# GpSimd's elementwise work during attention, whole tiles before and half tiles after

## The chip, the cores and the metric

The kernel runs on one core of a Trainium2 chip. The core has five engines with instruction queues of their own: TensorE (PE in the profile, its weight loads PEld), VectorE (DVE), ScalarE (ACT), GpSimd (POOL) and SyncE (SP, which here issues nearly all DMAs). Each engine works its queue in order, and engines wait for each other through semaphores. The metric is the device time of one launch in microseconds (us), lower is better.

## The reference, cut to what matters

Attention with a threshold, and then two dense layers, each with an activation of its own, all in float32:

```
scores = q @ k.T / sqrt(64)                      # 4 batches, 8 heads, 576 x 576, head size 64
keep   = scores >= max(scores, -1) - tau
attn   = exp(scores - max) * keep ;  attn /= sum(attn, -1) + 1e-9
x      = (attn @ v)  -> (2304, 512)
h      = x @ w_in  (512 x 2048);   g = where(h >= 1, h, where(h <= -1, 0, (h + 1)**2 / 4));  y = g @ w_out
h      = y @ w_in2 ;               g = h * clip(h + 3, 0, 6) / 6 ;                           out = g @ w_out2
```

## The kernel before, in words

Attention is cut into 16 jobs, one for each batch and pair of heads, and a job into five blocks of query rows. For a block TensorE multiplies `kt` and `qt` into two PSUM banks (L328). VectorE moves each bank to SBUF as `p` and takes the row maximum on the way (L341). ScalarE takes the exponential `e` (L353). VectorE forms the threshold `th` (L356), and multiplies `e` by the mask into `p`, with the row sum as a second output (L362, the instruction with two SBUF inputs that returns throughout the text). TensorE transposes `p` (L277), ScalarE evicts the transposed tiles (L390, L404), and TensorE multiplies them by `v` (L426). When a job is over, VectorE takes the reciprocals of its row sums (L445, L446, L449), these go through DRAM to come back broadcast as `rb`, and GpSimd multiplies the job's output `xu` by `rb` (L481). From the fifth job on q and k are transposed by VectorE (L286, L302), and GpSimd scales the transposed queries by 0.125 (L288).

Every float32 weight is split into a high and a low part that TensorE takes in a fast format, and a product is three matmuls. The split of one 128x512 weight tile goes through three engines in turn: ScalarE (L118, L121), GpSimd clamps (L122), VectorE shifts (L129) and joins signs (L135), GpSimd adds the integer parts (L137), ScalarE rounds to the high part (L139), GpSimd subtracts to get the low part (L141). While attention runs, 20 such tiles are split.

After the first batch's four jobs the first dense layer begins on the finished columns, interleaved with the remaining attention. A step of it is twelve matmuls (L666) into a bank, ScalarE's L675 and L676, VectorE's L677 (one PSUM and one SBUF input) into `r`, ScalarE's rounding `gh` (L683), GpSimd's `gl` (L684), and twelve matmuls with the outgoing weights (L728). When attention is over, the rest of the first layer and the second one follow, in wider tiles (L666 and L708).

The order on each engine isn't written by hand: the program is recorded, and a list scheduler with a model of each instruction's time lays the queues out, within the dependences, a few priorities, and added dependences ("after") that keep some pace. What one instruction is thought to take thus moves others, on all engines.

Of the kernel before, what the change touches and what calls it, by code (L numbers as in the profile page):

```python
# [11 lines left out]
ALU = mybir.AluOpType  # L12
U32 = mybir.dt.uint32
I32 = mybir.dt.int32
# [4 lines left out]
def kernel(  # L19
# [13 lines left out]
    V, S, G, T = nc.vector, nc.scalar, nc.gpsimd, nc.tensor  # L33
    NB, NH, SEQ, D = q.shape
# [29 lines left out]
    taus = const.tile([128, 4], F32, name="taus")  # L64
# [9 lines left out]
    def f32(ap):  # L74
        return ap.bitcast(F32)
# [26 lines left out]
    def after(ins, prev, sync=False):  # L102
        if prev is not None:
            kind = mybir.DependencyClass.Sync if sync else mybir.DependencyClass.NoSync
            why = mybir.DependencyReason.ANTI if sync else mybir.DependencyReason.DATA
            tc.add_manual_dep(ins.ins, prev.ins.name, mybir.DependencyInfo(kind, why), reason="pace")

    pe_pins = []
    pins = {"S": None, "V": None, "G": None}

    def split_a(kind, m, f):
        t = wraw.pop((kind, m, f))
        pool = wbase if f < NF1 else wpool[f]
        hi = pool.tile([128, 512], F32R, tag=f"w{kind}h{f}", name=f"w{kind}h{f}")
        lo = pool.tile([128, 512], F32R, tag=f"w{kind}l{f}", name=f"w{kind}l{f}")
        c = stage.tile([128, 512], U32, tag="w_c", name="w_c", bufs=2)
        r = t[:, :, 0].bitcast(I32)
        x = S.activation(out=r, in_=t[:, :, 0], func=ACTF.Copy, scale=2.0 ** -29)  # L118
        after(x, pins["S"])
        if mode["att"]:  # L120
            after(S.activation(out=f32(c), in_=f32(t[:, :, 1]), func=ACTF.Abs), x)  # L121
            G.tensor_scalar(  # L122
                out=f32(c), in0=f32(c), scalar1=122879.9921875, scalar2=2.0 ** -15, op0=ALU.min, op1=ALU.max)
        else:
            S.activation(out=f32(c), in_=f32(t[:, :, 1]), func=ACTF.Abs)
            x = V.tensor_scalar(
                out=f32(c), in0=f32(c), scalar1=2.0 ** -15, scalar2=122879.9921875, op0=ALU.max, op1=ALU.min)
            after(x, pins["V"])
        V.tensor_scalar(out=c, in0=c, scalar1=3, scalar2=0x3FFFFFFF,  # L129
                        op0=ALU.logical_shift_left, op1=ALU.bitwise_and)  # L130
        wc[kind, m, f] = (hi, lo, c, t, r)

    def split_b(kind, m, f):
        hi, lo, c, t, r = wc.pop((kind, m, f))
        V.scalar_tensor_tensor(out=c, in0=t[:, :, 1], scalar=0xC0000000, in1=c,  # L135
                               op0=ALU.bitwise_and, op1=ALU.bitwise_or)
        x = G.tensor_tensor(out=c.bitcast(I32), in0=c.bitcast(I32), in1=r, op=ALU.add)  # L137
        after(x, pins["G"])
        x = S.activation(out=hi, in_=f32(c), func=ACTF.Copy)  # L139
        after(x, pins["S"])  # L140
        x = G.tensor_tensor(out=lo, in0=f32(c), in1=f32(hi), op=ALU.subtract)  # L141
        after(x, pins["G"])
        wsp[kind, m, f] = (hi, lo)

    wc = {}
# [1 line left out]
    class Weights:  # L147
# [16 lines left out]
        def half(self):  # L164
            if self.done < len(self.items):
                it = self.items[self.done]
                if not self.mid:
                    self.prefetch()
                    split_a(*it)
                else:  # L170
                    split_b(*it)
                    self.done += 1
                    self.prefetch()
                self.mid = not self.mid
# [32 lines left out]
    mode = {"mlp": False, "att": True, "step": False, "t": 0, "s": 0, "n": 0}  # L207
# [4 lines left out]
    qt, kt = {}, {}  # L212
# [17 lines left out]
    def load_q(j):  # L230
        if j >= NJ:
            return
        E = nc.sync if j else nc.scalar
        b, hp = jobs[j]
        for h in HEADS:
            src = q[b, 2 * hp + h]
            if j >= JT:
                strips(qn, 0, src, h)
                continue
            E.dma_start(out=qn[:, 0:4, h * D:(h + 1) * D], in_=rows(src, b))  # L240
            E.dma_start(out=qn[0:TAIL, 4, h * D:(h + 1) * D], in_=src[MAIN:SEQ, :])
# [15 lines left out]
    def load_v(j):  # L257
        if j >= NJ:
            return
        b, hp = jobs[j]  # L260
        t = vn[j % 2]
        for h in HEADS:
            src = v[b, 2 * hp + h]
            nc.sync.dma_start(out=t[:, 0:4, h, :], in_=rows(src, b))
            nc.sync.dma_start(out=t[h * TAIL:(h + 1) * TAIL, 4, h, :], in_=src[MAIN:SEQ, :])
# [3 lines left out]
    def unit_bank():  # L269
        mode["s"] += 1  # L270
        return pair_bank(f"P{mode['s'] % 2}")

    def reads(x, ago=0):
        readers[(mode["s"] - ago) % 2] = x

    def turn(out, in_, pin):
        x = T.transpose(out, in_, ident)  # L277
        if pin:
            pe_pins.append(x)

    def unit_q(j):
        if j >= NJ or j in qt:
            return
        qt[j] = ap.tile([128, SEQ], F32, tag="qt", name="qt", bufs=2)
        if j >= JT:
            V.transpose(out=qt[j], in_=qn.rearrange("p c n -> p (c n)")[:, 0:SEQ])  # L286
            load_q(j + 1)
            G.tensor_scalar(out=qt[j], in0=qt[j], scalar1=taus[:, 1:2], scalar2=None, op0=ALU.mult)  # L288
            return
        tm = unit_bank().rearrange("p e n -> p (e n)")  # L290
        for c in range(5):
            turn(tm[:, c * 128:(c + 1) * 128], qn[:, c, :], c == 0)
        load_q(j + 1)
        reads(S.activation(out=qt[j], in_=tm[:, 0:SEQ], func=ACTF.Copy, scale=taus[:, 1:2]))
# [118 lines left out]
    def pv_chunk():  # L413

        j, g, c = pvq.pop(0)
        n, d0 = GROUPS[g]
        f, t = gt[g, j]
        if c == 0:
            if j not in xu:
                here.pop(j - XLIVE, None)  # L420
                xu[j] = here[j] = mt.tile([128, SEQ], F32, tag="xu", name="xu", bufs=XLIVE)
            o_t[j, g] = rotate() if mode["mlp"] else bank("Q1")
        o = o_t[j, g][:, 0:n]
        for h in (1, 0):
            with tc.high_priority(offset=0 if h else 900):
                mm = T.matmul(o[h * D:(h + 1) * D], vn[j % 2][:, c, h, :], f[:, h, c] if c < 4 else t,  # L426
                              start=(c == 0), stop=(c == 4), skip_group_check=True)
            after(mm, pe_pins[-1] if h else prev)
            prev = mm
        if c == 4:  # L430
            del gt[g, j], o_t[j, g]
            S.activation(out=xu[j][:, d0:d0 + n], in_=o, func=ACTF.Copy)
# [38 lines left out]
    def em_norm(j):  # L471
        if j not in rbs:
            return
        while any(x[0] == j for x in pvq):
            pv_chunk()
        b, hp = jobs[j]
        rz, rb = rbs.pop(j)
        if j in OVER:
            load_v(j + 2)
            x = xu.pop(j)  # L480
            G.tensor_tensor(out=x, in0=x, in1=rb, op=ALU.mult)  # L481
            done_jobs.add(j)
            if b < NB - 1:
                nc.sync.dma_start(out=xd[b][:, hp, :], in_=x[:, 0:MAIN])
            nc.sync.dma_start(out=xd[NB][:, hp, b * TAIL:(b + 1) * TAIL], in_=x[:, MAIN:SEQ])
            return
        bm = unit_bank().rearrange("p e n -> p (e n)")
        for c in range(4):
            T.transpose(bm[:, c * 128:(c + 1) * 128], rb[:, c].rearrange("p h n -> p (h n)"), ident)
        load_v(j + 2)  # L490
        bt = bm[:, 512:640]
        T.transpose(bt, rz[:, 8, :].to_broadcast([128, 128]), ident)
        x = xu.pop(j)
        reads(V.tensor_tensor(out=x[:, 0:MAIN], in0=x[:, 0:MAIN], in1=bm[:, 0:MAIN], op=ALU.mult))
        done_jobs.add(j)
        if b < NB - 1:
            nc.sync.dma_start(out=xd[b][:, hp, :], in_=x[:, 0:MAIN])
        for h in HEADS:
            r = slice(64 * h, 64 * h + 64)
            reads(V.tensor_tensor(out=x[r, MAIN:SEQ], in0=x[r, MAIN:SEQ], in1=bt[r, 64 * h:64 * h + 64], op=ALU.mult))  # L500
        nc.sync.dma_start(out=xd[NB][:, hp, b * TAIL:(b + 1) * TAIL], in_=x[:, MAIN:SEQ])
# [3 lines left out]
    def attention():  # L505
# [36 lines left out]
        for t in range(n + 6):  # L542
            mode["t"] += 1
            mode["step"] = True
            if not mode["mlp"]:
# [18 lines left out]
                for x in now_at("q"):  # L564
                    unit_q(*x)
                    yield
# [15 lines left out]
            else:  # L582
# [18 lines left out]
                for x in now_at("q"):  # L601
                    unit_q(*x)
                    yield
# [186 lines left out]
    while o < len(outs):  # L790
        n = len(steps)
# [138 lines left out]
    for _ in attention():  # L930
# [11 lines left out]
        while credit > 0:  # L942
            c = next(part1)
# [98 lines left out]
```

## Time and profile before

| | us |
|---|---|
| median of 3 runs | 1124.85 (1124.29 to 1128.67) |
| the profiled execution | 1126.53 |
| its span | 1124.7 |
| PE busy in the span | 1086.1 |
| DVE, ACT, POOL busy | 586.9, 614.3, 435.5 |

The span is what the trace covers; 1.8 us of the profiled execution lie around it, and the execution itself is 1.7 us over the median. PE is busy 97% of the span, and the 40-slice picture shows where it isn't: in the first eight slices (some 225 us) it stands at 7 to 9 tenths, while DVE stands at 7 to 9 as well, and from there to the last slice it is full. The granted clock is full except in parts of those first slices.

### The profile page before, as it was taken

To read this page: it belongs to the slowest core of one execution; us is meant where nothing else is said; L and a number is where in the kernel's file an instruction comes from. 1 tells how busy PE (TensorE), PEld (TensorE's weight loads), DVE (VectorE), ACT (ScalarE), POOL (GpSimd) and SP (SyncE) were. 2 spreads that over 40 slices of the span, in tenths; PEclk is the share of its full clock that TensorE was granted. 3 is DMA by queue.
4 is the path that set the end of the run, shared out by engine and by line. 5 is a ranking of instruction groups with operands and counts; after the bars stand their busy time and mean duration, and the time that the engine had idled before them with its cause. 6 is when DMAs were issued, how large, how long until landed. Compare 5 with 4: busy or idle time off the path is not lost.

```text
span 1124.7 us, 17618 instructions
## 1 busy us (share of the span) xinstructions
PE 1086.1 (97%) x6478; PEld 881.8 (78%) x6478; DVE 586.9 (52%) x1204; ACT 614.3 (55%) x1215; POOL 435.5 (39%) x382
## 2 busy tenths in 40 slices
PE   7988779999999999999999999999999999999998
PEld 5555557778887778888889888888888888898886
DVE  5788979876666666256535855657410211211111
ACT  5677777776666666565657766645422322333222
POOL 1133667632212221246636666568622222222221
PEclk9999999999999999999999999999999999999999
DMA  6353535433222210015322444543110110010001
GB/s 166 95 117 79 135 102 157 121 73 87 63 59 64 55 39 24 12 49 169 94 85 85 132 147 153 153 128 102 35 38 1 34 38 1 10 38 6 14 1 38
DMA packets 140422, 84.26 MB, mean 75 GB/s; under 512 B 99632, under 2 KB 123440, under 8 KB 140336
## 3 DMA queue, kind: packets, MB, share of 16 engines
q1 hardware_dynamic: 138976, 82.84, 26.8%
q8 instruction: 51, 0.84, 0.3%
q10 hardware_dynamic: 1360, 0.30, 0.1%
q14 instruction: 35, 0.29, 0.1%
HBM read 65.73 MB, written 17.37 MB: 74 GB/s over the span
## 4 chain that ended last, share of the span: by engine, by line
PE 86%; DVE 6%; ACT 3%; DMA 2%; issue 1%; POOL 1%; SPq 1%; ACTq 0%; DVEq 0%; POOLq 0%
PE Q L666 35%; PE P L708 28%; PE Q L728 7%; PE P L328 6%; PE Q L426 5%; PE Q L277 5%; DVE p L341 2%; DVE p L362 2%; ACT e L353 1%; DMA qn<-in_q_dram 1%; DMA w_raw<-in_moe_w_in_dram 0%; DMA rb<-rd 0%; DVE w_c L135 0%; ACT Gf L390 0%; SPq L227 0%
## 5 line engine op out<-in xcount | busy, mean ns | idle before, releaser
L684 POOL TENSOR_TENSOR gl<-r,gh 128x512 fp32r<-128x512 f32 (+1 forms) x190 | 202.4, 1065 | 508.3 <-ACT gh L683 506.4
L666 PE MATMUL Q<-xh,wih 128*128 128x512 f32 (+1 forms) x760 | 262.7, 346 | 6.9 <-DVE r L677 6.0
L666 PE MATMUL Q<-xh,wil 128*128 128x512 f32 (+1 forms) x760 | 257.6, 339 | 0.0
L666 PE MATMUL Q<-xl,wih 128*128 128x512 f32 (+1 forms) x760 | 257.5, 339 | 0.0
L680 DVE SCALAR_TENSOR_TENSOR r<-r,Q 128x512 f32<-128x512 f32 (+1 forms) x80 | 50.7, 634 | 249.3 <-ACT r L679 249.2
L683 ACT ACTIVATE gh<-r 128x512 fp32r<-128x512 f32 (+1 forms) x190 | 99.9, 526 | 128.5 <-PE P L708 52.3
L666 PEld LDWEIGHTS Q<-xh,wih 128*128 128x128 f32 x760 | 144.6, 190 | 31.4 <-DVE r L677 8.2
L666 PEld LDWEIGHTS Q<-xl,wih 128*128 128x128 f32 x760 | 144.6, 190 | 15.8
L666 PEld LDWEIGHTS Q<-xh,wil 128*128 128x128 f32 x760 | 144.5, 190 | 15.3
L341 DVE TENSOR_SCALAR_CACHE_REDUCE p<-P 128x576 f32<-128x576 f32 x144 | 103.9, 751 | 54.4 <-PE Q L277 39.1
L362 DVE SCALAR_TENSOR_TENSOR p<-p,th,e 128x576 f32<-128x576 f32 x144 | 123.6, 879 | 15.4 <-ACT e L353 9.6
L679 ACT ACTIVATE r<-Q,three 128x512 f32<-128x512 f32 (+1 forms) x80 | 51.5, 643 | 143.7 <-PE Q L666 140.5
L353 ACT ACTIVATE e<-p,nm 128x576 f32<-128x576 f32 x144 | 108.5, 774 | 29.2 <-DVE p L341 28.3
L677 DVE SCALAR_TENSOR_TENSOR r<-r,Q 128x256 f32<-128x256 f32 (+1 forms) x110 | 54.9, 499 | 120.2 <-ACT r L676 117.0
L277 PE MATMUL Q<-ident,p 128*128 128x128 f32 x656 | 108.5, 284 | 7.8 <-ACT Gf L390 4.3
L328 PE MATMUL P<-kt,qt 64*128 64x288 f32 (+1 forms) x640 | 99.4, 429 | 14.7 <-DVE p L341 13.8
L708 PE MATMUL P<-woh,gh 128*128 128x512 f32 x288 | 111.9, 390 | 0.6 <-DVE ob L766 0.6
L708 PE MATMUL P<-wol,gh 128*128 128x512 f32 x288 | 112.2, 390 | 0.0
L708 PE MATMUL P<-woh,gl 128*128 128x512 f32 x288 | 111.0, 390 | 0.0
L277 PEld LDWEIGHTS Q<-ident,p 128*128 128x128 f32 x656 | 74.5, 142 | 44.2 <-issue 11.8
L137 POOL TENSOR_TENSOR w_c<-w_c,w_raw 128x512 int32<-128x512 int32 x64 | 88.7, 1387 | 41.7 <-DVE w_c L135 21.8
L390 ACT ACTIVATE Gf<-Q 128x512 f32<-128x512 f32 x128 | 74.2, 595 | 34.4 <-PE Q L277 33.6
(91 smaller groups left out, 1834.3 us busy)
## 6 DMA issues: line engine op xcount, KB each, us to landing
w_raw<-in_moe_w_in_dram SPq DMA_DIRECT2D x32, 512.0 KB
w_raw<-in_moe_w_out_dram SPq DMA_DIRECT2D x32, 512.0 KB
vn<-in_v_dram SPq DMA_DIRECT2D x32, 128.0 KB
x2p<-ob SPq DMA_DIRECT2D x16, 256.0 KB
x2d<-ob SPq DMA_DIRECT2D x16, 256.0 KB
xst<-x2d SPq DMA_DIRECT2D x16, 256.0 KB
out_dram<-ob SPq DMA_DIRECT2D x16, 256.0 KB
xst<-xd SPq DMA_DIRECT2D x15, 256.0 KB
```

Of the source, the lines that this page charges most:

```text
L137: x = G.tensor_tensor(out=c.bitcast(I32), in0=c.bitcast(I32), in1=r, op=ALU.add)
L277: x = T.transpose(out, in_, ident)
L328: mm = T.matmul(o, qt[j][r, c], kt[j][r, k0:k0 + HS], start=True, stop=True, skip_group_check=True)
L341: reads(V.tensor_scalar(out=p[:, x], in0=s[:, :, 0:HS], scalar1=-1.0, scalar2=3e38, op0=ALU.mult, op1=ALU.min, accum_out=nm[:, x:x + 1]), ...
L353: pins["S"] = S.activation(out=e, in_=p[:, x], func=ACTF.Exp, bias=nm[:, x:x + 1], scale=-1.0)
L362: V.scalar_tensor_tensor(out=p[:, x], in0=p[:, x], scalar=th[:, x:x + 1], in1=e, op0=ALU.is_le, op1=ALU.mult, accum_out=zt[j][:, z:z + 1])
L390: S.activation(out=f[:, h, :, d0:d0 + 128], in_=tm.rearrange("p (c n) -> p c n", c=4), func=ACTF.Copy)
L666: mm = T.matmul(h, l[:, kk * 128:(kk + 1) * 128], r, start=(x == 0), stop=(x == 3 * KD - 1))
L683: x = S.activation(out=gh, in_=r, func=ACTF.Copy)
L684: y = G.tensor_tensor(out=gl, in0=r, in1=f32(gh), op=ALU.subtract)
L708: T.matmul(a, l, r, start=(first and x == 0), stop=(last and x == 2))
L728: mm = T.matmul(o, l, r, start=(f == fs[0] and x == 0 and i == 0), stop=(f == fs[-1] and x == 2 and i == 1), skip_group_check=True)
```

## The change

Four kinds of GpSimd instruction are issued as two instructions of half the columns each, as long as attention runs: the integer add and the subtraction of the weight split, the scaling of the queries, and the product with the reciprocal sums. Their operands, the arithmetic and the engine stay; the clamp (L122), `gl` (L684) and all work after attention stay whole.

```diff
+    def halves(n):
+        w = n // 2 if mode["att"] else n
+        return [slice(a, a + w) for a in range(0, n, w)]
...
-        x = G.tensor_tensor(out=c.bitcast(I32), in0=c.bitcast(I32), in1=r, op=ALU.add)
-        after(x, pins["G"])
+        for s in halves(512):
+            x = G.tensor_tensor(out=c.bitcast(I32)[:, s], in0=c.bitcast(I32)[:, s], in1=r[:, s], op=ALU.add)
+            after(x, pins["G"])
         x = S.activation(out=hi, in_=f32(c), func=ACTF.Copy)
         after(x, pins["S"])
-        x = G.tensor_tensor(out=lo, in0=f32(c), in1=f32(hi), op=ALU.subtract)
-        after(x, pins["G"])
+        for s in halves(512):
+            x = G.tensor_tensor(out=lo[:, s], in0=f32(c)[:, s], in1=f32(hi)[:, s], op=ALU.subtract)
+            after(x, pins["G"])
...
-            G.tensor_scalar(out=qt[j], in0=qt[j], scalar1=taus[:, 1:2], scalar2=None, op0=ALU.mult)
+            for s in halves(SEQ):
+                G.tensor_scalar(out=qt[j][:, s], in0=qt[j][:, s], scalar1=taus[:, 1:2], scalar2=None, op0=ALU.mult)
...
-            G.tensor_tensor(out=x, in0=x, in1=rb, op=ALU.mult)
+            for s in halves(SEQ):
+                G.tensor_tensor(out=x[:, s], in0=x[:, s], in1=rb[:, s], op=ALU.mult)
```

In the changed kernel's listing the lines are higher: L129 is L133, L135 is L139, L137 is L142, L141 is L147, L288 is L295, L341 is L348, L356 is L363, L362 is L369, L481 is L489, L650 is L658, L677 is L685.

On GpSimd the order is mostly the old one with each split instruction written twice. This is the stretch in the middle of the weight splits, before:

```order
L481 TENSOR_TENSOR xu<-xu,rb 128x576
L137 TENSOR_TENSOR w_c<-w_c,w_raw 128x512
L141 TENSOR_TENSOR wil_1438<-w_c,wih_1437 128x512
L684 TENSOR_TENSOR gl<-r,gh 128x256
L141 TENSOR_TENSOR wol_1501<-w_c,woh_1500 128x512
L122 TENSOR_SCALAR w_c<-w_c 128x512
L288 TENSOR_SCALAR qt<-qt,taus 128x576
```

And after:

```order
L489 TENSOR_TENSOR xu<-xu,rb 128x288 x2
L142 TENSOR_TENSOR w_c<-w_c,w_raw 128x256 x2
L147 TENSOR_TENSOR wil_1453<-w_c,wih_1452 128x256 x2
L692 TENSOR_TENSOR gl<-r,gh 128x256
L147 TENSOR_TENSOR wol_1518<-w_c,woh_1517 128x256 x2
L126 TENSOR_SCALAR w_c<-w_c 128x512
L295 TENSOR_SCALAR qt<-qt,taus 128x288 x2
```

The two halves stand directly behind each other, with nothing between them in GpSimd's own queue.

VectorE's order is the old one, but for a few swaps of neighbours, until the fourth transposition of queries (some 135 us into the trace); from there the scheduler lays it out anew. This is the piece that ran at 163 to 173 us, with two steps of the weight split, two masks and one activation of the dense layer, before:

```order
L129 TENSOR_SCALAR w_c<-w_c 128x512
L356 TENSOR_SCALAR th<-nm,taus 128x2
L135 SCALAR_TENSOR_TENSOR w_c<-w_raw,w_c 128x512
L362 SCALAR_TENSOR_TENSOR p,z<-p,th,e 128x576 x2
L677 SCALAR_TENSOR_TENSOR r<-r,Q_1809 128x256
L129 TENSOR_SCALAR w_c<-w_c 128x512
L135 SCALAR_TENSOR_TENSOR w_c<-w_raw,w_c 128x512
```

And the piece that answers to it after the change:

```order
L133 TENSOR_SCALAR w_c<-w_c 128x512
L658 TENSOR_TENSOR xl<-xu,xh 128x256
L363 TENSOR_SCALAR th<-nm,taus 128x2
L139 SCALAR_TENSOR_TENSOR w_c<-w_raw,w_c 128x512
L685 SCALAR_TENSOR_TENSOR r<-r,Q_1646 128x256
L369 SCALAR_TENSOR_TENSOR p,z<-p,th,e 128x576 x2
L133 TENSOR_SCALAR w_c<-w_c 128x512
L139 SCALAR_TENSOR_TENSOR w_c<-w_raw,w_c 128x512
```

The dense layer's activation has moved ahead of the two masks, and a split of the dense layer's input has come in. Counted over the queue, the dense layer's activations that VectorE has done when it comes to the fifth transposition of queries are 8 before and 6 after, at the sixth 14 and 13, at the seventh 19 and 18, and from the tenth on they are the same.

## Rows read from the trace of the kernel before

**Rows 1.** Busy time by stretch: start:end, length, then each engine's busy us, PEclk.

```profile
0.00:110.00 110.00, 94.17 (x641) 59.36 (x642) 84.69 (x230) 75.63 (x152) 26.26 (x34) 0.97 0.50 116
110.00:235.00 125.00, 106.62 (x782) 82.35 (x779) 110.45 (x239) 96.57 (x212) 81.14 (x71) 0.97 0.47 121
235.00:1120.00 885.00, 884.43 (x5059) 739.72 (x5056) 391.79 (x737) 441.36 (x852) 328.14 (x277) 1.00 0.22 63
130.00:160.00 30.00, 21.85 (x142) 17.54 (x142) 23.33 (x51) 21.67 (x47) 20.65 (x19) 0.89 0.48 125
160.00:190.00 30.00, 26.09 (x198) 19.84 (x197) 28.68 (x56) 23.93 (x53) 22.27 (x20) 1.00 0.50 129
```

**Rows 2.** Waits of PE, 0 to 250 us: total us, times, longest us.

```profile
PE P L328 <- DVE p L341: 13.8, 15, 2.7
PE Q L666 <- DVE r L677: 6.0, 4, 2.1
```

**Rows 3.** Groups of DVE instructions, 0 to 232 us: count, busy us, mean ns, idle.

```profile
L362 DVE SCALAR_TENSOR_TENSOR p<-p,th,e 128x576 f32<-128x576 f32 x76 | 69.4, 934 | 7.9 <-ACT e L353 4.9 <-DVE th L356 0.5
...
L135 DVE SCALAR_TENSOR_TENSOR w_c<-w_raw,w_c 128x512 uint32<-128x512 uint32 x20 | 16.8, 842 | 0.2
L356 DVE TENSOR_SCALAR th<-nm,taus 128x2 f32<-128x2 f32 (+1 forms) x42 | 13.4, 318 | 0.9
L129 DVE TENSOR_SCALAR w_c<-w_c 128x512 uint32<-128x512 uint32 x20 | 12.5, 627 | 0.2 <-POOL w_c L122 0.2
```

**Rows 4.** The same groups, 10 to 42 us, where POOL is nearly idle.

```profile
L362 DVE SCALAR_TENSOR_TENSOR p<-p,th,e 128x576 f32<-128x576 f32 x15 | 11.9, 817 | 1.4 <-ACT e L353 0.7
L356 DVE TENSOR_SCALAR th<-nm,taus 128x2 f32<-128x2 f32 (+1 forms) x8 | 1.8, 227 | 0.3
...
L135 DVE SCALAR_TENSOR_TENSOR w_c<-w_raw,w_c 128x512 uint32<-128x512 uint32 x1 | 0.7, 686 | 0.0
L129 DVE TENSOR_SCALAR w_c<-w_c 128x512 uint32<-128x512 uint32 x1 | 0.4, 417 | 0.0
```

**Rows 5.** Timelines of DVE, POOL and PE around 127 us: start us, duration us.

```profile
125.74 1.85 DVE L362 SCALAR_TENSOR_TENSOR p<-p,th,e 128x576 f32<-128x576 f32 x1
...
127.52 1.95 DVE L362 SCALAR_TENSOR_TENSOR p<-p,th,e 128x576 f32<-128x576 f32 x1
...
125.43 1.55 POOL L137 TENSOR_TENSOR w_c<-w_c,w_raw 128x512 int32<-128x512 int32 x1 [0.63 <-DVE w_c L135]
127.14 1.72 POOL L481 TENSOR_TENSOR xu<-xu,rb 128x576 f32<-128x576 f32 x1 [0.17 <-ACT xu L432]
...
130.47 0.38 PE L666 MATMUL Q<-xh,wih 128*128 128x256 f32 x1 [1.66 <-DVE r L677]
```

**Rows 6.** Timelines of DVE and POOL around 168 us.

```profile
166.83 1.82 DVE L362 SCALAR_TENSOR_TENSOR p<-p,th,e 128x576 f32<-128x576 f32 x1
...
168.59 0.41 DVE L677 SCALAR_TENSOR_TENSOR r<-r,Q 128x256 f32<-128x256 f32 x1
...
166.25 1.79 POOL L137 TENSOR_TENSOR w_c<-w_c,w_raw 128x512 int32<-128x512 int32 x1 [0.70 <-DVE w_c L135]
168.01 1.12 POOL L122 TENSOR_SCALAR w_c<-w_c 128x512 f32<-128x512 f32 x1
```

**Rows 7.** Timeline of DVE, the first and the last of the 28 blocked instructions.

```profile
42.93 1.04 DVE L650 TENSOR_TENSOR xl<-xu,xh 128x256 fp32r<-128x256 f32 x1 [2.17 <-ACT xh L649]
...
225.77 1.85 DVE L362 SCALAR_TENSOR_TENSOR p<-p,th,e 128x576 f32<-128x576 f32 x1
```

**Rows 8.** Timeline of POOL, a 512-column and a 256-column instruction without contention.

```profile
152.91 1.29 POOL L137 TENSOR_TENSOR w_c<-w_c,w_raw 128x512 int32<-128x512 int32 x1 [2.41 <-DVE w_c L135]
...
187.52 0.74 POOL L684 TENSOR_TENSOR gl<-r,gh 128x256 fp32r<-128x256 f32 x1 [2.75 <-ACT gh L683]
```

**Rows 9.** Waits of ACT, 0 to 250 us: total us, times, longest us.

```profile
ACT xh L649 <- POOL xu L481: 4.8, 3, 2.7
...
ACT woh L139 <- POOL w_c L137: 4.0, 4, 1.7
```

## The prediction

> **What bounds the kernel now.** I read the busy times by stretch first, to find where TensorE stands idle at all. From 235 us to 1120 us it is busy 884.4 of 885 us [rows 1]: nothing that VectorE or GpSimd does in the remaining attention or in the dense layers can shorten that part, as long as TensorE stays fed. Ahead of it, TensorE is idle 15.8 us of the first 110 and 18.4 us of the next 125 [rows 1]. In the second stretch VectorE is busy 110.5 of 125 us, 88%, ScalarE 77%, GpSimd 65%: VectorE is the engine that paces it. The waits of TensorE say the same: 13.8 us of them end on VectorE's eviction of the scores, L341, which frees the PSUM bank, and 6.0 us in only four waits end on the dense layer's activation, L677 [rows 2].
>
> The next question is what makes VectorE so busy there. I compared the mean duration of each of its instructions with the same instruction between 10 and 42 us, where GpSimd has almost no work. The mask, L362, takes 934 ns against 817; L135 842 against 686; L356 318 against 227; L129 627 against 417 [rows 3, 4]. Times their counts (76, 20, 42, 20) that is 8.9 + 3.1 + 3.8 + 4.2 = 20.0 us that VectorE spends inside instructions without getting on. The timeline shows how. At 125.43 us GpSimd starts L137, at 125.74 VectorE starts a mask, and the mask takes 1.85 us, ending 0.6 us after L137 does; the next one meets L481 and takes 1.95 [rows 5]. So an instruction of this kind does nothing until GpSimd's instruction has ended, and then runs its whole length. TensorE's wait of 1.66 us at 130.47 stands right behind this pair [rows 5].
>
> Laying the two timelines over each other from 0 to 232 us, 28 of VectorE's long instructions stand behind a GpSimd instruction that the change splits, the first at 42.93 and the last at 225.77 us [rows 7]; their excess adds up to 22.5 us (other instructions than the four groups are in it). That is the time which the change can touch.
>
> **The change part by part.** *The price on GpSimd.* A 512-column instruction takes 1.29 us, a 256-column one 0.74 [rows 8]: two halves are 1.48 us, 0.19 us more. Until 232 us there are 20 adds, 20 subtractions, 6 query scalings and 6 products, 52 splits, so 9.9 us on GpSimd. The scaling and the product at 288 columns aren't in the trace; I take the same 0.19 for them, between nothing and the whole of a 256-column instruction, 0.74, and for 12 of them this is 2.3 us between 0 and 8.9. GpSimd has 44 us idle in the busy stretch [rows 1], which covers it; the splits after 235 us (six scalings, eight products) lie beside a full TensorE and cost nothing.
>
> *What waits for the second half.* ScalarE's rounding waits for all of L137, its splitting of `xu` for all of L481: 4.0 us in four waits and 4.8 us in three [rows 9]. Each gets 0.19 us longer, and, when VectorE slips in between the halves, by what VectorE does there, at most the 0.82 us of a mask. With one in three so, a wait grows by 0.19 + 0.27 = 0.46 us, seven of them by 3.2 us. ScalarE is idle 28 of 125 us there [rows 1], so I let a quarter reach the end: +0.8 us, with 0 and +3.2 as bounds.
>
> *What VectorE gets.* An instruction that arrives in the first half waits for that half only, which for the add and the subtraction is 0.74 instead of 1.29 us from the start, a gain of up to 0.55. One that arrives in the second half gains nothing and loses the 0.1 to 0.2 us by which that half ends later. Replaying the 28 with halves of 0.70 to 0.90 us, every gain counted, gives 8.1 us. But the second half is then waiting in GpSimd's queue, and the next VectorE instruction that needs the same access finds it running. The trace has the case: L481 starts at 127.14, while the first mask still runs; it takes 1.72 us, and it is the second mask that is blocked, for over a microsecond [rows 5]. So the two engines take turns, and with halves VectorE merely pays for the second half one instruction later. The gain stays only where the instruction behind the blocked one doesn't need that access: L677 at 168.59, with one input from PSUM, takes its usual 0.41 us [rows 6], and L341, which reads PSUM, and the transpositions run undisturbed too. Of the 28, 8 are followed by such instructions, and keep 3.0 us together (0.38 us each); 6 arrive late, and lose 0.5 us; 14 are followed by another mask, threshold or shift, and come out at nothing. That is 2.5 us, with 8.1 as the upper bound; the lower bound is a loss of 0.19 us at each of the 28 blocks, 5.3 us, if VectorE never gets in. I take 2.5 since the pairs in rows 5 are the commonest pattern. As VectorE paces this stretch, I count the whole of it.
>
> The Trainium skill's page "SBUF — State Buffer", section "SBUF: two separate sides", says that the port pair which the two engines share is an exclusive lock for the whole instruction, and that the loser blocks fully. The trace agrees that a block lasts until the other's end [rows 5]. By this rule alone halves would halve every block, 11 us; it leaves open who comes next, which the same rows show.
>
> *What the new order moves.* Up to some 135 us VectorE's queue is the old one, but behind the fourth transposition it is laid out anew, and the dense layer falls behind attention: 6 activations instead of 8 at the fifth transposition, 13 instead of 14 at the sixth. Work of TensorE that filled stretches paced by VectorE moves towards those where TensorE is full. TensorE does 198 matmuls in 26.1 busy us there, 0.13 us each [rows 1], so a step's first twelve are 1.6 us, and with one step late where saturation begins I charge half of it, +0.8 us, since the piece that answers to 163 to 173 us has the activation ahead of the two masks, where TensorE's four waits for L677 lie. The bounds come from the two halves of this stretch: 130 to 160 us is idle 8.2 of 30 us at a mean granted clock of 0.89, 160 to 190 only 3.9 of 30 at 1.00 [rows 1]. If the second went like the first, +4.2 us, and as 0.89 is 6.6 us at the lower level (1.2 of 2.4 GHz), which loses 3.3 us, together +7.5; if the first went like the second, the same saved.
>
> *The sum.* -2.5 + 0.8 + 0.8 = -0.9 us. Against the profiled execution, 1126.53 us, this is 1125.6; on the scale of the median, which is 1.7 us lower, 1124.85 - 0.9 gives 1123.9 us.
>
> **The rivals.** *The blocks really halve* (faster). VectorE keeps the whole 8.1 us, because the second half often falls beside L341 or an idle moment in the new order. For it: several of TensorE's waits, as that of 1.66 us, stand directly behind a blocked pair [rows 5]. Against it: half the blocked instructions are followed by another of their kind. 1124.85 - 8.1 + 0.8 = 1117.5 us; with the clock's 3.3 us kept as well, 1114.2.
>
> *The new order is worse* (slower). The scheduler doesn't know the blocking and lays out 135 to 235 us anew with attention further ahead. It decides where 160 to 190 us comes out like 130 to 160: 1124.85 + 7.5 + 0.8, less 1.0 us for the turns that are kept in the rest of the stretch, gives 1132.2 us.
>
> *GpSimd doesn't let VectorE in between two instructions that are both ready* (no change, or slower). Then each of the 28 blocks lasts 0.19 us longer: 1124.85 + 5.3 + 0.8 = 1131.0 us. Against it: L137 at 166.25 and L122 behind it have no gap, yet the mask that started at 166.83 ended at 168.65, and L122 took 1.12 us, so the mask ran between them [rows 6]. The Trainium skill's "GPSIMD Engine Reference", section "Instruction dispatch", states that each GpSimd core begins the next instruction as soon as it is through with its own share; if that kept the access taken across two halves, this case would hold. The trace speaks against it in the one pair named.
>
> *Everything is taken back by turns* (no change): 0 from VectorE, +0.8 and +0.8: 1126.4 us.
>
> **How the numbers follow.** The forecast, 1123.9 with its own range of 1120.5 to 1127, has 0.37; blocks that halve 0.24; all taken back 0.16; the worse order 0.15; no turn at all 0.08. A measurement of this kernel can tell 0.5%, 5.6 us, from no change, so faster is below 1119.2 and slower above 1130.5. Faster gets the 0.24 and 0.02 of a better order, 0.26. Slower gets 0.12 of the worse order, which may fall short of its price, and 0.06 of the no-turn case, 0.18. The rest is 0.56. The range leaves out about 0.07 below and 0.1 above: 1115 to 1131.
>
> **What would show it.** In the profile after, the add and subtraction should show 40 instructions each of some 0.73 us at 256 columns while attention runs. If the turns hold, L362's mean before 232 us stays above 880 ns, and masks with 1.4 to 1.5 us take the place of those with 1.85; if the blocks halve, it falls to 870 or below. If VectorE doesn't get in, masks of 2 us appear. TensorE's idle time from 110 to 235 us should stay within 3 us of 18.4; if it falls below 13 the gain is larger than I think, above 24 the new order is at fault. I am wrong too if anything behind 235 us changes, or if the waits of ScalarE for GpSimd grow by more than 3.2 us.

## The result and the profile after: slower by 0.6%

| | before | after |
|---|---|---|
| median, us | 1124.85 (1124.29 to 1128.67) | 1131.85 (1130.66 to 1134.27, 5 runs) |
| the profiled execution, its span, us | 1126.53, 1124.7 | 1131.61, 1129.8 |
| PE, DVE, ACT, POOL busy, us | 1086.1, 586.9, 614.3, 435.5 | 1088.2, 584.4, 614.7, 455.5 |

The ratio is 1.0058, with a 95% interval from 1.0036 to 1.008. The prediction, 1123.9 us within 1115 to 1131, was wrong: the time lies above its range and in its "slower", which had 0.18.

The busy times by stretch after, with the columns of [rows 1]:

```profile
0.00:110.00 110.00, 91.15 (x618) 57.95 (x618) 82.29 (x223) 72.69 (x146) 27.01 (x45) 0.95 0.49 116
110.00:235.00 125.00, 107.45 (x780) 81.67 (x779) 107.76 (x238) 97.02 (x211) 95.17 (x111) 0.97 0.46 120
235.00:1120.00 885.00, 884.33 (x5063) 738.67 (x5062) 393.05 (x742) 443.76 (x858) 333.03 (x293) 1.00 0.21 63
160.00:190.00 30.00, 25.65 (x190) 19.46 (x187) 21.55 (x45) 21.43 (x50) 25.19 (x31) 0.97 0.50 130
```

A large part of the loss lies where I had no term for it. From 110 to 235 us TensorE is idle 17.6 us, not 18.4, and has done as many matmuls as before (780 and 782). But in the first 110 us it is idle 18.9 instead of 15.8 us [rows 1], and has done 618 matmuls instead of 641. What waits there is seen in the waits of TensorE, 0 to 250 us (total us, times, longest), which answer to [rows 2]:

```profile
PE P L335 <- DVE p L348: 8.7, 13, 1.5
PE Q L433 <- ACT Gf L397: 7.8, 4, 3.3
PE Q L283 <- ACT Gf L397: 6.1, 11, 1.4
PE Q L283 <- ACT Gt L415: 4.4, 1, 4.4
PE Q L674 <- DVE r L685: 2.7, 3, 1.5
```

The waits for VectorE fell, from 13.8 to 8.7 us and from 6.0 to 2.7. In their place stand more waits for evictions by ScalarE: those for Gf are 13.9 us, and 4.4 us for a Gt are new. Before, in the same view, Gf had 5.9 us:

```profile
PE Q L277 <- ACT Gf L390: 4.3, 5, 2.1
...
PE Q L426 <- ACT Gf L390: 1.6, 1, 1.6
```

And these are the waits of ScalarE itself, answering to [rows 9]:

```profile
ACT xh L657 <- POOL xu L489: 7.8, 3, 3.5
...
ACT woh L144 <- POOL w_c L142: 4.1, 5, 1.2
...
ACT w_raw L122 <- DMA w_raw<-in_moe_w_out_dram: 2.6, 1, 2.6
...
ACT w_raw L122 <- DMA w_raw<-in_moe_w_in_dram: 1.4, 1, 1.4
```

The waits of `woh` for the add's second half are what they were (4.1 us, 4.0 before; those of `wih`, which [rows 9] don't show, fell from 2.0 to 0.2). The three waits for the product grew from 4.8 to 7.8 us, and ScalarE now stands 4.0 us before weights that haven't landed, where it stood 1.2. The first of the three, in the timelines of GpSimd, ScalarE and TensorE of the changed kernel (start us, duration us):

```profile
40.19 1.54 POOL L489 TENSOR_TENSOR xu<-xu,rb 128x288 f32<-128x288 f32 x2 [10.60 <-DMA rb<-rd]
...
37.93 0.58 ACT L397 ACTIVATE Gf<-Q 128x512 f32<-128x512 f32 x1
41.01 0.42 ACT L657 ACTIVATE xh<-xu 128x256 fp32r<-128x256 f32 x1 [2.51 <-POOL xu L489]
41.33 0.58 ACT L397 ACTIVATE Gf<-Q 128x512 f32<-128x512 f32 x1
41.81 0.27 ACT L411 ACTIVATE Gt<-Q 128x128 f32<-128x128 f32 x1
...
41.97 2.28 PE L433 MATMUL Q<-Gf,vn 128*64 128x256 f32 x12 [2.17 <-ACT Gf L397]
```

The rounding `xh` stands at the head of ScalarE's queue for 2.51 us, until the first half of the product is through, which itself waited for the reciprocal sums' DMA. The eviction at 41.33 is behind it, and TensorE waits for that one. Before, ScalarE did the same eviction first and let the rounding wait afterwards, for 2.73 us: this first wait is no longer than it was, but now the eviction stands behind it. ScalarE's queue at this place, with what the change moved marked:

```diff
 L390 Gf<-Q
+L649 xh<-xu
 L390 Gf<-Q
 L404 Gt<-Q
 L353 e<-p,nm
 L139 wih<-w_c
-L649 xh<-xu
```

The rounding moved four places ahead; the second moved six, the third two. The other two waits are 3.46 us (to 63.33 us; 0.19 before) and 1.82 us (to 87.20; 1.89 before), and TensorE's waits for Gf behind them 3.32 and 1.81 us. `xh` of the first column group reads columns 0 to 255, so it depends on the half from 0 to 287 alone, and to the scheduler it seemed ready earlier. Two orders laid out without a run speak for this: cut at 288, whichever half is written first, the scheduler puts the half from 0 first and the roundings move ahead; cut at 64, so that `xh` needs both pieces, they stay at their old places.

What VectorE pays, in its groups from 0 to 232 us, as [rows 3]:

```profile
L369 DVE SCALAR_TENSOR_TENSOR p<-p,th,e 128x576 f32<-128x576 f32 x74 | 68.0, 943 | 6.0 <-ACT e L360 3.1
L139 DVE SCALAR_TENSOR_TENSOR w_c<-w_raw,w_c 128x512 uint32<-128x512 uint32 x20 | 17.6, 878 | 0.2
L363 DVE TENSOR_SCALAR th<-nm,taus 128x2 f32<-128x2 f32 (+1 forms) x41 | 13.2, 321 | 0.9
L133 DVE TENSOR_SCALAR w_c<-w_c 128x512 uint32<-128x512 uint32 x20 | 11.0, 551 | 0.0
```

Against the undisturbed 817, 686, 227 and 417 ns [rows 4] the excess is 9.3 + 3.8 + 3.9 + 2.7 = 19.7 us; it was 20.0. How the two engines share is plain in the timeline around 130 us, VectorE's rows ahead of GpSimd's:

```profile
129.39 1.29 DVE L369 SCALAR_TENSOR_TENSOR p<-p,th,e 128x576 f32<-128x576 f32 x1
130.62 0.08 DVE L369 DVE_READ_ACCUMULATOR p<-p,th,e 128x1 f32 x1
130.62 1.28 DVE L369 SCALAR_TENSOR_TENSOR p<-p,th,e 128x576 f32<-128x576 f32 x1
131.83 0.08 DVE L369 DVE_READ_ACCUMULATOR p<-p,th,e 128x1 f32 x1
131.83 1.27 DVE L139 SCALAR_TENSOR_TENSOR w_c<-w_raw,w_c 128x512 uint32<-128x512 uint32 x1
...
129.08 2.20 POOL L142 TENSOR_TENSOR w_c<-w_c,w_raw 128x256 int32<-128x256 int32 x2 [0.63 <-DMA rb<-rd]
131.24 2.52 POOL L489 TENSOR_TENSOR xu<-xu,rb 128x288 f32<-128x288 f32 x2
```

Where one mask took 1.85 us behind one whole instruction [rows 5], three instructions in a row now take 1.3 us, each behind a half, and a pair of halves lasts 2.2 to 2.5 us.

### The profile page after: what moved, and what is told of

Read it like the earlier page. It is cut to its first block, busy times and chain, and to the rows that moved or that the text cites. A ratio compares the mean times of both kernels' runs of the same rounds, so it can differ in the third digit from the quotient of the medians.

```text
span 1129.8 us, 17708 instructions
## 1 busy us (share of the span) xinstructions
PE 1088.2 (96%) x6478; PEld 882.0 (78%) x6478; DVE 584.4 (52%) x1204; ACT 614.7 (54%) x1215; POOL 455.5 (40%) x448
## 4 chain that ended last, share of the span: by engine, by line
PE 78%; DVE 6%; ACT 4%; DMA 4%; POOL 3%; issue 3%; SPq 1%; ACTq 0%; DVEq 0%; POOLq 0%
PE Q L674 31%; PE P L716 25%; PE Q L736 6%; PE P L335 6%; PE Q L433 5%; PE Q L283 4%; POOL w_c L142 2%; DVE p L348 2%; DMA rb<-rd 1%; DVE p L369 1%; POOL gl L692 1%; ACT Gf L397 1%; DVE w_c L139 1%; DVE r L685 1%; DVE w_c L133 1%
## 5 line engine op out<-in xcount | busy, mean ns | idle before, releaser
L692 POOL TENSOR_TENSOR gl<-r,gh 128x512 fp32r<-128x512 f32 (+1 forms) x190 | 204.7, 1078 | 506.8 <-ACT gh L691 501.7
L369 DVE SCALAR_TENSOR_TENSOR p<-p,th,e 128x576 f32<-128x576 f32 x144 | 124.5, 886 | 14.9 <-ACT e L360 8.8
L348 DVE TENSOR_SCALAR_CACHE_REDUCE p<-P 128x576 f32<-128x576 f32 x144 | 104.1, 752 | 51.2 <-PE Q L283 36.1
L685 DVE SCALAR_TENSOR_TENSOR r<-r,Q 128x256 f32<-128x256 f32 (+1 forms) x110 | 54.9, 500 | 125.6 <-ACT r L684 121.8
L142 POOL TENSOR_TENSOR w_c<-w_c,w_raw 128x512 int32<-128x512 int32 (+1 forms) x84 | 94.5, 1135 | 34.6 <-DVE w_c L139 14.9
```

Of the source, the lines that this page charges most:

```text
L142: x = G.tensor_tensor(out=c.bitcast(I32)[:, s], in0=c.bitcast(I32)[:, s], in1=r[:, s], op=ALU.add)
L348: reads(V.tensor_scalar(out=p[:, x], in0=s[:, :, 0:HS], scalar1=-1.0, scalar2=3e38, op0=ALU.mult, op1=ALU.min, accum_out=nm[:, x:x + 1]), ...
L369: V.scalar_tensor_tensor(out=p[:, x], in0=p[:, x], scalar=th[:, x:x + 1], in1=e, op0=ALU.is_le, op1=ALU.mult, accum_out=zt[j][:, z:z + 1])
L692: y = G.tensor_tensor(out=gl, in0=r, in1=f32(gh), op=ALU.subtract)
```

## The experiments

Two things change together: the halves, and the order in which the scheduler lays out all queues. To part them, every engine's queue can be held to a given order by dependences that add no wait (instruction after instruction on the same engine). "Old order" is that of the kernel before, "new order" that of the changed kernel. Laid out without a run and held to its own order, the kernel before comes out as the same program, so the holding adds nothing. Ratios are to the kernel before, run again beside each experiment (medians from 1124.32 to 1126.08 us), with 95% intervals; differences in us are such a ratio times 1124.85. Of the code, only the line that matters is shown.

**Halves in the old order.** The changed kernel, held to the order before, each pair of halves in the place of the whole.

```diff
+    pin_order(tc, old_order)
```

> The changed kernel's half-column GpSimd instructions, with every engine's queue held in the order of the kernel before (the two halves where the whole one stood). Theory 'order' (the slowdown of 7.0 us comes from the queues that the scheduler laid out anew, and the halves by themselves are worth nothing, since VectorE and GpSimd take turns): 1123 to 1127 us, ratio 0.998 to 1.002. Theory 'halves' (longer GpSimd work and second halves that block VectorE cost the time): 1130 to 1133 us. My forecast's own term for VectorE, -2.5 us, and +0.8 for the waits of ScalarE would give 1123.2 us here.

Measured: 1122.72 us, 0.9975 [0.9962, 0.9989]. So the halves by themselves, in the old order, make the kernel faster, by 2.8 us. VectorE's groups, 0 to 232 us, in this run:

```profile
L379 DVE SCALAR_TENSOR_TENSOR p<-p,th,e 128x576 f32<-128x576 f32 x77 | 68.6, 912 | 9.4 <-ACT e L370 6.3 <-DVE th L373 0.5
L147 DVE SCALAR_TENSOR_TENSOR w_c<-w_raw,w_c 128x512 uint32<-128x512 uint32 x20 | 16.2, 809 | 0.2
L373 DVE TENSOR_SCALAR th<-nm,taus 128x2 f32<-128x2 f32 (+1 forms) x43 | 14.3, 333 | 0.9
L141 DVE TENSOR_SCALAR w_c<-w_c 128x512 uint32<-128x512 uint32 x20 | 11.3, 563 | 0.9 <-POOL w_c L134 0.9
```

Their excess is 7.3 + 2.5 + 4.6 + 2.9 = 17.3 us, 2.7 less than before. But a second thing changed, and it bears on what the 2.8 us came from. ScalarE's waits for the product, 4.8 us in three before:

```profile
ACT xh L667 <- POOL xu L499: 1.7, 1, 1.7
```

In the old places the rounding, which needs the first half only, starts earlier than before (41.88, 60.82 and 79.96 us against 42.48, 62.13 and 83.11), and the first matmul of the dense layer comes at 107.84 us instead of 112.39. The waits for the add grew meanwhile, `woh` and `wih` together from 6.0 to 9.1 us.

**Whole instructions in the new order.** The kernel before, held to the order of the changed one.

```diff
+    pin_order(tc, new_order)
```

> The kernel before, all GpSimd instructions whole, with every engine's queue held in the order of the changed kernel. Theory 'order': 1130 to 1134 us, as the changed kernel. Theory 'halves': 1124 to 1126 us. If the two add up, this and the run with halves in the old order share the 7.0 us between them.

Measured: 1139.47 us, 1.0116 [1.01, 1.0131]. The order alone costs 13 us, and the halves give half of it back. TensorE's waits for Gf in L429 (the L426 of before) are 11.5 us in four, ScalarE's three waits for the product 11.5 us.

**The three roundings earlier, nothing else.** The kernel before in the old order, with its first three `xh` ahead on ScalarE as in the changed kernel (the first is the piece of queue shown above).

> The kernel before, in its own order, but for three instructions: ScalarE's first three roundings of the dense layer's input (xh from xu) stand 4, 6 and 2 places earlier in ScalarE's queue, where the changed kernel has them. All else as before. Theory 'order, by ScalarE's wait for xu': these three, which wait for a product that comes late from a DMA, hold up the exponentials and evictions behind them, and cost the 3.0 to 3.3 us by which the first dense matmul comes later in the changed kernel: 1127 to 1129 us. Rival 'order, by TensorE's own queue' (the products with v and the transpositions changed places): 1124 to 1126 us.

Measured: 1141.35 us, 1.0122 [1.0105, 1.014]. Three instructions of 0.4 us, moved by 4, 6 and 2 places, cost 13.7 us, more than I gave them and, within the intervals, no less than the whole new order with whole instructions. ScalarE's and TensorE's waits in this run:

```profile
ACT xh L652 <- POOL xu L484: 15.0, 3, 7.2
```

```profile
PE P L331 <- DVE p L344: 12.2, 16, 1.5
PE Q L429 <- ACT Gf L393: 11.9, 2, 7.0
PE Q L280 <- ACT Gf L393: 5.8, 7, 2.9
```

Attention is behind from there on: the first matmul of the dense layer comes at 127.46 us, against 112.39 before and 115.73 in the changed kernel.

TensorE's clock has a part in this. After its wait of 7.02 us sixteen matmuls took 3.64 us, at a granted clock of 0.52, the lower level; a group of the same form took 1.95 us in the kernel before, at 38.47 us, with TensorE at work just ahead and the clock at 1.00:

```profile
71.71 3.64 PE L429 MATMUL Q<-Gf,vn 128*64 128x256 f32 x16 [7.02 <-ACT Gf L393]
```

**The three roundings later.** The same kernel, `xh` 12 places later on ScalarE and `xl` 12 later on VectorE.

> The kernel before, in its own order, but the same three roundings stand 12 places later in ScalarE's queue, and the three subtractions that follow them (xl) 12 places later in VectorE's. They are needed only by the first dense step at 112 us. If ScalarE's and VectorE's waits for this product count (4.8 us of ScalarE, of which the waits of TensorE at 46 us, 2.06, and 84 us, 1.55, are the trace): 1120 to 1123 us. If they are hidden anyway: 1124 to 1126 us.

Measured: 1122.73 us, 0.997 [0.9956, 0.9983]; ScalarE has no wait for the product, and the first dense matmul comes at 107.97 us. So the 4.8 us in [rows 9], which stood in the kernel before, had a price too, about 3.4 us. VectorE's excess did not fall in this run. The largest of its groups:

```profile
L365 DVE SCALAR_TENSOR_TENSOR p<-p,th,e 128x576 f32<-128x576 f32 x78 | 74.1, 972 | 8.8 <-ACT e L356 5.6 <-DVE th L359 0.5
```

Over the four groups it is 22.8 us, 2.8 more than before, in a kernel that is 3.4 us faster.

**The changed kernel with the roundings put back.** Held to the new order, `xh` later by 4, 6 and 2 places.

> The changed kernel, with every queue held to the order that it has there, but the first three roundings xh of the dense layer's input put back on ScalarE's queue by 4, 6 and 2 places, to where they stood before the change. Theory (these three alone make the change slow): the loss goes, 1122 to 1126 us, TensorE's first dense matmul falls back from 115.7 to some 108 to 112 us, and its waits for the evictions Gf from 7.8 to under 3 us. Rival (the rest of the new order, from 135 us on, costs too): it stays at 1128 to 1131.

Measured: 1127.44 us, 1.0024 [1.0014, 1.0034], from 1.0058: 3.8 us of the loss go, and the time lies between my theory and the rival. My theory that these three alone make the change slow fell here, as against the old order (0.9975) 5.5 us are left. Its waits of TensorE, 110 to 250 us, show the next one:

```profile
PE Q L293 <- ACT Gt L425: 4.5, 1, 4.5
PE P L345 <- DVE p L358: 3.5, 5, 1.5
PE Q L293 <- ACT Gf L407: 2.9, 5, 1.3
```

and ScalarE's timeline what it waited for:

```profile
148.46 0.65 ACT L130 ACTIVATE w_raw<-w_raw 128x512 int32<-128x512 uint32 x1 [2.65 <-DMA w_raw<-in_moe_w_out_dram]
149.02 0.64 ACT L133 ACTIVATE w_c<-w_raw 128x512 f32<-128x512 f32 x1
149.56 0.40 ACT L667 ACTIVATE xh<-xu 128x256 fp32r<-128x256 f32 x1
...
152.59 0.45 ACT L425 ACTIVATE Gt<-Q 64x64 f32<-64x64 f32 x2
```

It is the same pattern at another place: a step of the weight split waits 2.65 us at the head of the queue for its DMA, and the eviction for which TensorE waits is nine instructions behind it.

**Everything in halves but the product,** queues laid out freely.

```diff
-            for s in halves(SEQ):
-                G.tensor_tensor(out=x[:, s], in0=x[:, s], in1=rb[:, s], op=ALU.mult)
+            G.tensor_tensor(out=x, in0=x, in1=rb, op=ALU.mult)
```

> The change without its last part: the product with the reciprocal sums stays whole, conversions and query scaling are halved, and the queues are laid out freely. Their order is then the old one up to some 135 us, the three roundings at their old places. Theory (it is the split product that moves the roundings): 1121 to 1126 us, like before or a little faster. Rival (the halved conversions, or the order behind 135 us, cost as well): 1128 us or more.

Measured: 1128.59 us, 1.0027 [1.0015, 1.0039]. The roundings are at their old places (three waits for the product, 5.3 us), so it is the product's split that moves them; but the order behind differs again, ScalarE stands 2.1 and 2.1 us before weights, and no gain is left. The time is the rival's, though the roundings are where the theory put them.

**The product alone in halves,** the rest whole, queues laid out freely.

> The kernel before with the product alone in two halves, and the queues laid out freely; the three roundings then move ahead by 4, 6 and 2 places as in the changed kernel. Theory: slower than before, 1131 to 1141 us, and above the whole change, since no other halves give something back. Rival (the loss comes from the halved conversions): 1124 to 1127 us.

Measured: 1132.69 us, 1.0067 [1.0054, 1.008]. One of the four edits brings the whole loss; it can't be told from the whole change (1.0058). VectorE's excess in this run is 17.2 us, as low as with all halves in the old order.

**The roundings back, and two steps of the weight split later.** Beside xh_back, the pair of one tile (below) and the L122 of another.

```diff
-L122 w_raw<-w_raw
-L125 w_c<-w_raw
 L657 xh<-xu
...
 L415 Gt<-Q
 L400 Gf<-Q
+L122 w_raw<-w_raw
+L125 w_c<-w_raw
```

> The changed kernel in its own order, with the three roundings put back as in xh_back, and two steps of the weight split moved behind the evictions that wait behind them on ScalarE: L122 and L125 of the tile that keeps ScalarE waiting 2.55 us for its DMA at 153.7 us, ten places later, and the L122 that waits 1.42 us at 169.1, seven places later. Theory (what is left of the loss in xh_back, 5.5 us against the old order, is mostly ScalarE standing before weights that have not landed, with evictions behind): TensorE's 4.4 us wait for the eviction Gt goes, 1122 to 1125 us. Rival (it is the order of the dense layer against attention, or the clock, and the wait only moves): 1126 to 1128 us, as xh_back.

Measured: 1123.26 us, 0.9989 [0.9979, 0.9998], 3.9 us below xh_back. TensorE's wait for this Gt fell from 4.5 to 0.7 us. What is left to the old order (0.9975) lies within the intervals.

**Only the two steps later,** `xh` left ahead.

> The changed kernel in its own order, with only the same two steps of the weight split moved later on ScalarE, and the three roundings left ahead. Theory: the two losses lie in different stretches and add up; 1127 to 1129 us, 3 to 4 below the changed kernel. Rival (a later weight keeps TensorE waiting just as long): 1131 to 1133 us.

Measured: 1129.89 us, 1.005 [1.0035, 1.0064]; unclear. The Gt wait is gone here too, but ScalarE's three waits for the product are 9.8 us instead of 7.8, and what was won behind 135 us was lost ahead of 110, where the queues of the two kernels are the same. Whether those 2 us are chance isn't settled.

**Halves in the old order, and the roundings 12 places later.**

> All four kinds of GpSimd instruction in halves, every queue held to the order before the change, but the three roundings xh 12 places later on ScalarE and the subtractions xl 12 later on VectorE. If what halves save (2.8 us in the old order) and what later roundings save (3.4 us) come from different waits: 1119 to 1121 us. If both take away the same waits of ScalarE for the product: 1122 to 1124 us.

Measured: 1122.16 us, 0.9968 [0.9956, 0.998], the fastest of all and faster than both kernels, but not told apart from either edit alone (0.9975, 0.997): the two gains don't add up. This is the second of the two cases above, in which both take away the same waits of ScalarE for the product. Against the roundings 12 places later alone, the halves lower VectorE's excess from 22.8 to 18.2 us, and the ratio goes from 0.997 to 0.9968, 0.2 us; the intervals leave room for some 2 us either way.

## Why the prediction was wrong

- *What the new order moves* is the step that failed. "Up to some 135 us VectorE's queue is the old one" is true, and I took it for the order of the whole kernel. ScalarE's queue changes at some 40 us, where `xh` moves ahead, and I never compared it. I charged +0.8 us for the order; held to it with whole instructions, the kernel loses 13 us, and with halves the changed order costs 9.3 us (0.9975 to 1.0058). Of these, 3.8 are the three roundings and, with them back, 3.9 the two steps of the weight split; 1.6 us are left within the intervals. By themselves the two steps bring only 0.9 us, within the interval.
- *What waits for the second half* was reckoned with ScalarE's instructions in their old places, at most +3.2 us, and for the product the sign was wrong even there: the rounding needs the first half only, and its waits fell from 4.8 to 1.7 us, while those for the add grew from 6.0 to 9.1 (two of them, 2.0 us of `wih`, I had not counted). In the new order the waits for the product grew by 3.0 us, not because a second half came later, but because the rounding came to the head of the queue earlier. Nor did I count what is queued behind it; there the evictions stand for which TensorE waits.
- *What VectorE gets*, -2.5 us, came out as a number in the old order: the excess fell by 2.7 us, the time by 2.8. That the one made the other is not shown, and the runs speak against it, so I count this as luck too. The excess does not go with the time: it is 22.8 us at a ratio of 0.997, 18.2 at 0.9968, and 17.2 at 1.0067. The 2.8 us go rather with the shorter waits of ScalarE for the product: with the roundings out of the way, the halves bring nothing that can be told from zero. "As VectorE paces this stretch, I count the whole of it" is thus a second step that failed. In the new order the excess fell by 0.3 us only.
- *The turns* themselves are seen directly (1.29, 1.28 and 1.27 us in a row), and L369 stays above 880 ns, as foretold. The masks took 1.3 us rather than the 1.4 to 1.5 that I named, and the adds are 40, as foretold, but of 882 ns on average instead of 730. My reading that a blocked mask "runs its whole length" after GpSimd's instruction was too strict: in [rows 5] both masks end 0.6 us after it, and a mask alone takes 0.82.
- *The rivals.* "The new order is worse" gave 1132.2 us, near the 1131.85 measured, but by another mechanism: from 160 to 190 us TensorE is idle 4.4 us against 3.9, which is not the +4.2 that I had priced. I count the number as luck. "The blocks really halve" and "GpSimd doesn't let VectorE in" are refuted for VectorE's instructions by the excess (17.3 us in the old order, where they would leave 11.9 and 25.3) and by the turns.
- *The sign I set up* was TensorE's idle time from 110 to 235 us, "above 24 the new order is at fault". It is 17.6 us, and the order is at fault all the same: with its roundings ahead of 110 us, where I had no term, and behind 135 us with weights that ScalarE waits for, which I had not read either.
- Not settled: why the same three places cost 13.7 us with whole instructions in the old order and 3.8 with halves in the new one. In the one, ScalarE's waits for the product are 15.0 us, in the other 7.8. Nor is the clock's part in the prices known. The median of the granted clock over a whole run is 0.985 with the three roundings early and 0.992 in the kernel before, run beside it; it is 0.991 in the changed kernel, 0.995 with the roundings back, and 0.997 with the two weight steps later as well. If TensorE were the limit wherever the clock is low, these differences would be worth 7.9 us where 13.7 were measured, 4.5 where 3.8 were, and 2.3 where 3.9 were (upper bounds, estimated as the difference times 1125 us). That the moved instructions cause the loss is shown; how much of it is waiting, and how much the lower clock behind the waits, is not.

## What to carry to other kernels

An edit that changes what a scheduler sees has two prices, that of the instructions and that of the order, and the second must be read on every engine's queue, the evicting engine first. Look in the new order for instructions that moved ahead and depend on a DMA or a slow neighbour, and then at what stands behind them. Holding the queues to one order parts the two: here -2.8 us for the edit, and +9.3 for what came with it. And when a saving has the forecast size, look for a second path before believing the first: here one run that took away the other path left nothing of it that could be measured.

## What was not expected of the hardware

A pair of 288-column halves that met VectorE's instructions took 2.52 us, where the whole took 1.72 in like company [rows 5]: GpSimd too waits its turn at each half. ScalarE did not pass over a waiting instruction: at 41.01 us an activation of 0.42 us kept ScalarE still for 2.51, while the eviction behind it had its operand from TensorE, which had been idle since 39.80.
